# Linear attention and an ELU network on one core: the third token group's attention moved from transposed products to row products and DMA transposes

## The chip, the core and the metric

The kernel runs on one core of a Trainium2 chip. The core has a matrix engine (TensorE, "PE" in profiles, with its weight loads as "PEld"), VectorE ("DVE"), ScalarE ("ACT"), GpSimd ("POOL") and SyncE ("SP"), which mostly issues DMAs. Each engine works through its own list of instructions in order and waits on semaphores for the others. SBUF is the working memory with 128 partitions; PSUM, where TensorE leaves its results, has eight banks of 128 x 512 float32. The metric is the device time of one execution in microseconds (us).

## What is computed

```python
def _attn_ref(q, k, v, g_norm):                # q, k, v: 8 batches, 8 heads, 576 rows, 64 columns
    kv = np.einsum('bhsd,bhse->bhde', k, v)
    out = np.einsum('bhsd,bhde->bhse', q, kv)
    rms = np.sqrt(np.mean(out * out, axis=-1, keepdims=True) + 1e-06)
    return (out / rms * g_norm).astype(np.float32)

def _moe_ref(x, w_in, w_out):                  # x: 4608 x 512, w_in: 512 x 2048, w_out: 2048 x 512
    h = x @ w_in
    g = np.where(h > 0.0, h, 1.0 * (np.exp(np.minimum(h, 0.0)) - 1.0))
    return (g @ w_out).astype(np.float32)
```

Per batch and head, a 64 x 64 state kv is formed, each row of q is multiplied by it and normed; the heads are put side by side into rows of 512, and a two-layer network with an ELU runs over the 4608 rows. Inputs and output are float32; the kernel multiplies in bfloat16.

## The kernel before

**Groups.** The 4608 rows are cut into nine groups T of 512 (batches have 576 rows, so group T needs batches up to T, and group 2 still uses the end of batch 1). For each group there is an attention part, which ends in `xT[T]` (512 columns of x on partitions in four chunks c, 512 rows), a first product, and a second product. `mm1(T, i, tag)` computes two of the 16 column blocks of h, eight matmuls over 512 columns, into a pair of PSUM banks named by its tag, and hands it to `elu`: ScalarE takes Exp of it (line 350), VectorE takes min(e, 1) - 1 (358) and the larger of that and h (362) into `gT[T]`. The second step, returned as `rest`, reads h from PSUM, so the pair is free only after it. With `relu` set, ScalarE also copies Relu(h) into an SBUF tile `elu_h`, the pair is free after that, and VectorE adds from SBUF. `mm2(T, j, f0, f1)` adds the blocks f0 to f1 of the second product for the 128 rows j; `mm2_half(T, i)` is eight of these matmuls, and the last of a row block copies it out on ScalarE (`mm2_out`, 415) and stores it through SP.

**PSUM.** Pairs "A" and "B" (two banks each), two single banks "m", and two banks that are "x" up to group 1's end and the pair "at" afterwards. Whoever takes over a bank waits until its last reader is done.

**Two kinds of attention.** Groups 0, 1 and 2 use the class `Turned`: q is transposed on TensorE (`turned_q`, `q_t_mm`, line 174) and copied to `qT`; the product y comes out transposed (`y_mm`, 189), is squared on ScalarE (229), summed over a head by a matmul with a block of ones (`mean_mm`, 199), turned into 1/rms by Ln and Exp over 512 columns (208, 209) and scaled by VectorE into `xT` (212). From group 3 on, `attention(T)` does it by rows, in named pieces: `kv` (state of batch T on TensorE, copy on ScalarE), `se0`/`se1` (row product of half a group into the pair "at", Square on ScalarE), `sum0`/`sum1` (reduce on VectorE, 283), `inv0`/`inv1` (Ln, Exp on 16 columns, ScalarE, 291 and 292), `mul0`/`mul1` (scale on VectorE into `xs`, 299, and two DMA transposes on SP into `xT`, 306), `gain0`/`gain1` (g_norm on VectorE, 312). For it, q is loaded as float32 into `st_q` (`fetch_ahead`), cast on GpSimd in six instructions (`cast_q`), and transposed by two DMAs on SP into `qT` (`turn_q`, 331). `after_turn` puts a small copy on GpSimd that waits for these transposes, so that the next batch's loads, issued by GpSimd, start after them.

**Order.** The order on each engine is the order of the program text. Group 1's attention is spread over group 0's second product. Group 1's first product (i = 0 to 7, on pairs m, B, A, B, A, B, A, B) has the pieces of group 2's attention between its column blocks (`pieces`), then four halves of group 1's second product with the rest of group 2's norms. From T = 2 on, `window` runs group T's first product with the pieces of group T+1's attention before (`early`) and after (`late`) an ELU's `rest`, and with halves of group T-1's second product (`second`).

Of the kernel before, what the change touches and what calls it, by code (L numbers as in the profile page):

```python
# [16 lines left out]
def kernel(  # L17
# [14 lines left out]
    P = 128  # L32
# [110 lines left out]
    def qT_tile(b):  # L143
        qT[b] = attp.tile([P, 2, 2, RK, 64], BF16, name="qT", tag="qT", bufs=3)
        return qT[b]

    def x_tile(T):
        xT[T] = attp.tile([P, KC, G], BF16, name="xT", tag="xT")
        return xT[T]

    def kv_mm(b, kv_ps, u, ls=range(2)):
        for j in range(RK):
            for s in range(2):
                rows = slice(s * 64, s * 64 + 64)
                for l in ls:
                    nc.tensor.matmul(  # L156
                        kv_ps[s][l * 64 : l * 64 + 64, u * 64 : u * 64 + 64],
                        lhsT=bf["k", b][rows, 2 * l + u, j, :],
                        rhs=bf["v", b][rows, 2 * l + u, j, :],
                        start=(j == 0),  # L160
                        stop=(j == RK - 1),
                    )
# [8 lines left out]
    def q_t_mm(b, u, js, dst):  # L171
        for n, j in enumerate(js):
            for l in range(2):
                nc.tensor.transpose(  # L174
                    dst[l * 64 : l * 64 + 64, n * P : n * P + P], bf["q", b][:, 2 * l + u, j, :], ident
                )
# [166 lines left out]
    def elu(T, i, ps, relu):  # L343

        parts = [(0, 2, ps)]
        if isinstance(ps, list):
            parts = [(a, a + 1, ps[a].unsqueeze(1)) for a in range(2)]
        e = mlpt.tile([P, 2, G], BF16, name="elu_e", tag="elu_e")
        for lo, hi, h in parts:
            nc.scalar.activation(e[:, lo:hi, :], h, AF.Exp)  # L350
        if relu:
            r = mlpt.tile([P, 2, G], BF16, name="elu_h", tag="elu_h", bufs=2)
            for lo, hi, h in parts:
                nc.scalar.activation(r[:, lo:hi, :], h, AF.Relu)
            parts = [(0, 2, r)]

        def rest():
            nc.vector.tensor_scalar(  # L358
                out=e, in0=e, scalar1=1.0, scalar2=1.0, op0=ALU.min, op1=ALU.subtract
            )  # L360
            for lo, hi, h in parts:
                nc.vector.tensor_tensor(  # L362
                    out=gT[T][:, 2 * i + lo : 2 * i + hi, :],
                    in0=e[:, lo:hi, :],
                    in1=h,
                    op=ALU.add if relu else ALU.max,
                )

        return rest

    def g_tile(T):
        gT[T] = mlpg.tile([P, FC, G], BF16, name="gT", tag="gT")
# [20 lines left out]
    o_ps, o_sb = {}, {}  # L393
# [107 lines left out]
    for name in "kvq":  # L501
        fetch(name, 1, 1)
    load_w_out(3)
    for u in range(2):
        for name in "qkv":
            fetch(name, 2, u)
    fetch_ahead(3)
    cast_q(3)

# [11 lines left out]
    def turned_q(b, u, tag):  # L521

        ps = as_bf16(single(tag, "qt_ps"))
        q_t_mm(b, u, range(8), ps)
        return ps
# [42 lines left out]
                stop=(c == KC - 1),  # L568
            )

    qT_tile(0)
    x_tile(0)
    g_tile(0)
    g_ps = pair("A", "g_ps")
# [72 lines left out]
    def mm2_all(f0, f1, js=(2, 3, 0, 1)):  # L647
        for f in range(f0, f1):
            for j in js:
                mm2(0, j, f, f + 1)  # L650
# [4 lines left out]
            o_ps[0, j0 + t] = ps[:, t, :]  # L655

    x_tile(1)
    qT_tile(1)
    for u in range(2):
        n = Turned(1, u)  # L660
        if u == 0:
            mm2_all(0, 4, (2, 3))
        kv_ps = [single("x", "kv_ps") for _ in range(2)]
        kv_mm(1, kv_ps, u)
        kv_out(1, kv_ps, u, (A, A))
        if u == 0:
            mm2_all(0, 4, (0, 1))
        main = turned_q(1, u, "m")
        q_t_out(1, u, V, main, slice(0, 8))
        ends = as_bf16(single("m", "qt_ps"))  # L670
        for t in range(2):
            q_t_mm(t, u, (8,), ends[:, t * P : t * P + P])
        for t in range(2):
            q_t_out(t, u, V, ends[:, t * P : t * P + P], slice(8, 9))
        mm2_all(*((4, 6), (10, 11))[u])
        n.product([single("x", "y_ps") for _ in range(2)])
        for l in range(2):
            n.square(l)
        mm2_all(*((6, 7), (11, 12))[u])
        for l in range(2):  # L680
            n.sums(l, single("m", "mean"))
            n.inv(l)
            n.scale(l)
        mm2_all(*((7, 10), (12, 15))[u])
    for js in ((2, 3), (0, 1)):
        for j in js:
            mm2(0, j, 15, 16, out=False)
        for j in js:
            mm2_out(0, j)

    qT_tile(2)
    x_tile(2)
    n2 = [Turned(2, 0), Turned(2, 1)]

    def late_kv(u, tag):
        kv_ps = pair(tag, "kv_ps")
        kv_mm(2, kv_ps, u)
        kv_out(2, kv_ps, u, (A, A))  # L700

    def late_q(u, tag):
        main = turned_q(2, u, tag)
        end = as_bf16(single(tag, "qt_ps"))
        q_t_mm(2, u, (8,), end[:, 0:P])
        q_t_out(2, u, A, main, slice(0, 8))
        q_t_out(2, u, V, end[:, 0:P], slice(8, 9))

    def late_y(u):
        n2[u].product(pair("xm"[u], "y_ps"))  # L710
        for l in range(2):
            n2[u].square(l)

    def late_norm(u, l):
        n2[u].sums(l, single("mx"[u], "mean"))
        n2[u].inv(l)
        n2[u].scale(l)

    pieces = {
        1: lambda: late_kv(0, "x"),  # L720
        2: lambda: late_kv(1, "m"),
        3: lambda: late_q(0, "x"),
        4: lambda: (late_q(1, "m"), turn_q(3), after_turn(3), fetch_ahead(4)),
        5: lambda: late_y(0),
        6: lambda: late_norm(0, 0),
        7: lambda: late_norm(0, 1),
    }
    for i, tag in enumerate("mBABABAB"):
        rest = mm1(1, i, tag)
        rest()  # L730
        if i in pieces:
            pieces[i]()
    for j, tag in enumerate("AB"):
        o_ps[1, j] = pair(tag, "o_ps")[:, 0, :]
    mm2_half(1, 0)
    late_y(1)
    mm2_half(1, 2)
    late_norm(1, 0)
    mm2_half(1, 1)
    late_norm(1, 1)  # L740
    mm2_half(1, 3)
    start_psum.close()
    ps_at = ctx.enter_context(tc.tile_pool(name="ps_at", bufs=1, space=bass.MemoryType.PSUM))

    def window(T, at, early, late, second):
        for i in range(8):
            rest = mm1(T, i, "AB"[i % 2])
            for name in early.get(i, ()):  # L750
                at[name]()
            if i in second:
                second[i]()
            rest()
            for name in late.get(i, ()):
                at[name]()

    for T in range(2, NT):
        at, early, late = {}, {}, {}
        if T + 1 < NT:  # L760
            at = attention(T + 1)
# [54 lines left out]
```

## Time and profile before

| | us |
|---|---|
| median of 14 runs | 292.06 (291.72 to 292.58) |
| the profiled execution's own time | 292.08 |
| its span in the profile | 290.3 |
| first product of group 1 begins | 48.92 |
| first product of group 2 begins | 75.53 |
| first product of group 3 begins | 101.91 |
| second products, matmuls (line 399), in the chain | 40% of the span |
| first products, matmuls (line 378), in the chain | 41% of the span |
| VectorE, add or maximum of the ELU (line 362), 74 instructions | 84.6 |
| ScalarE, Exp of the ELU (line 350), 77 instructions | 73.8 |

The beginnings are starts of the first matmul in TensorE's timeline. Matmul durations in the trace (379 ns for one of 512 columns) overlap; the pace of a row of them, 16 in 3.45 us, is the cost of each. "Idle before" in a timeline is the time in which the engine did nothing ahead of that instruction, with what ended it.

### The profile page before, as it was taken

What the parts mean: (1) busy time and instruction counts of PE and PEld (TensorE: products, weight loads), DVE (VectorE), ACT (ScalarE), POOL (GpSimd) and SP (SyncE); (2) the same over time, 40 slices, a digit from 0 to 9 for tenths busy, and PEclk for the clock granted to TensorE, in tenths of its full rate; (3) what the DMA queues carried; (4) which work ended last, traced back from release to release, by engine and by line L of the source; (5) the groups of instructions that cost most, each with busy time, mean ns of one, the idle gap of its engine ahead of it and who ended that gap; (6) DMA issues with size and microseconds to landing.
All of it is one profiled execution on the core that took longest, in us unless ns stands there. A gap on an engine that the chain in (4) does not pass through costs nothing.

```text
span 290.3 us, 5182 instructions
## 1 busy us (share of the span) xinstructions
PE 282.6 (97%) x2145; PEld 130.3 (45%) x2145; DVE 165.3 (57%) x223; ACT 141.9 (49%) x207; POOL 46.9 (16%) x85
## 2 busy tenths in 40 slices
PE   8999999999999999999999999999999999999994
PEld 3444444444444444444444444444444444444443
DVE  2349632776368747762776377636774776344600
ACT  4568357587555435543554255525552555343320
POOL 7643341404200022203400330000000000000000
PEclk9999999999999999999999999999999999999999
DMA  7999999997901299958925894442140215020222
GB/s 210 187 204 206 206 207 237 303 193 217 184 2 36 43 169 246 169 100 240 235 53 93 224 239 73 86 107 72 38 102 6 75 36 108 0 75 0 72 75 73
DMA packets 46332, 37.77 MB, mean 130 GB/s; under 512 B 26468, under 2 KB 40036, under 8 KB 46308
## 3 DMA queue, kind: packets, MB, share of 16 engines
q0 software_dynamic: 15312, 20.71, 36.4%
q1 hardware_dynamic: 30592, 16.19, 25.8%
q10 hardware_dynamic: 404, 0.53, 0.5%
q8 instruction: 17, 0.28, 0.4%
q14 instruction: 7, 0.06, 0.0%
HBM read 36.70 MB, written 9.44 MB: 159 GB/s over the span
## 4 chain that ended last, share of the span: by engine, by line
PE 92%; DVE 3%; ACT 3%; DMA 1%; issue 0%; DVEq 0%
PE h_ps L378 41%; PE o_ps L399 40%; PE h_ps L563 2%; PE at L250 2%; PE kv_ps L519 2%; PE qt_ps L174 1%; DVE gT L362 1%; PE at L156 1%; ACT elu_e L350 1%; PE kv_ps L156 1%; PE mean L199 1%; PE y_ps L189 1%; PE mean L519 1%; ACT rT L209 1%; ACT rT L208 1%; DMA out_dram<-o_sb 1%
## 5 line engine op out<-in xcount | busy, mean ns | idle before, releaser
L399 PE MATMUL o_ps<-w_out_sb,gT 128*128 128x512 bf16 x560 | 130.5, 379 | 0.5 <-DVE gT L362 0.5
L378 PE MATMUL h_ps<-xT,w_in_sb 128*128 128x512 bf16 x552 | 128.7, 379 | 0.8 <-DVE gT L362 0.6
L350 ACT ACTIVATE elu_e<-h_ps 128x1024 bf16<-128x1024 f32 (+1 forms) x77 | 73.8, 974 | 91.4 <-PE h_ps L378 89.0
L362 DVE TENSOR_TENSOR gT<-elu_e,h_ps 128x1024 bf16<-128x1024 bf16 (+1 forms) x74 | 84.6, 1149 | 7.2
L399 PEld LDWEIGHTS <-gT 128*128 128x128 bf16 x560 | 54.4, 98 | 66.4 <-issue 1.8
L378 PEld LDWEIGHTS <-w_in_sb 128*128 128x128 bf16 x552 | 52.3, 98 | 62.5 <-issue 1.7
L358 DVE TENSOR_SCALAR elu_e<-elu_e 128x1024 bf16<-128x1024 bf16 x72 | 31.0, 430 | 69.3 <-ACT elu_e L350 69.0
L415 ACT COPY o_sb<-o_ps 128x512 f32<-128x512 f32 x32 | 18.5, 588 | 18.8 <-PE o_ps L399 18.7
L103 POOL CAST q_bf<-st_q 128x384 bf16<-128x384 f32 x30 | 14.4, 522 | 26.6 <-DMA st_q<-in_q_dram 26.6
L212 DVE SCALAR_TENSOR_TENSOR xT<-y_ps,g_col,rT 128x512 bf16<-128x512 f32 (+1 forms) x14 | 9.2, 672 | 15.4 <-ACT rT L209 13.4
L283 DVE TENSOR_REDUCE ss<-sq 128x16 f32<-128x1024 bf16 x12 | 14.6, 1220 | 4.9 <-ACT sq L277 4.9
L299 DVE TENSOR_TENSOR xs<-at,ss 128x1024 bf16<-128x1024 f32 x12 | 14.6, 1218 | 0.0
L277 ACT ACTIVATE sq<-at 128x1024 bf16<-128x1024 f32 x12 | 12.3, 1028 | 1.0 <-PE at L250 1.0
L339 POOL COPY gate<-qT 1x32 bf16<-1x32 bf16 x4 | 0.8, 199 | 73.3 <-DMA qT<-q_bf 73.3
L90 POOL DMA_DIRECT2D k_bf<-in_k_dram x12 | 8.4, 700 | 5.5 <-PE qt_ps L174 2.1
L156 PEld LDWEIGHTS <-k_bf 64*64 64x64 bf16 x576 | 6.4, 107 | 6.3 <-issue 5.9
L90 POOL DMA_DIRECT2D v_bf<-in_v_dram x12 | 8.3, 692 | 5.7 <-DMA w_in_sb<-in_moe_w_in_dram 2.1
L208 ACT ACTIVATE rT<-mean,eps_col 128x512 f32<-128x512 f32 (+1 forms) x9 | 6.6, 731 | 2.3 <-PE mean L199 2.1
L229 ACT ACTIVATE sq<-y_ps 128x512 bf16<-128x512 f32 x8 | 4.3, 595 | 6.4 <-PE y_ps L189 6.4
L112 DVE COPY o_sb<-o_ps 128x256 f32<-128x256 f32 x1 | 0.4, 425 | 11.5 <-DMA out_dram<-o_sb 11.5
L312 DVE TENSOR_SCALAR xT<-xT,g_col 128x1024 bf16<-128x1024 bf16 x12 | 5.7, 479 | 1.7 <-DMA xT<-xs 1.7
L112 DVE COPY qT<-qt_ps 128x128 bf16<-128x128 bf16 (+1 forms) x10 | 3.7, 406 | 5.0 <-PE qt_ps L174 5.0
(56 smaller groups left out, 113.3 us busy)
## 6 DMA issues: line engine op xcount, KB each, us to landing
out_dram<-o_sb SPq DMA_DIRECT2D x24, 256.0 KB, 3.9
st_q<-in_q_dram POOLq DMA_DIRECT2D x5, 1152.0 KB, 7.4
k_bf<-in_k_dram POOLq DMA_DIRECT2D x5, 576.0 KB, 9.4
v_bf<-in_v_dram POOLq DMA_DIRECT2D x5, 576.0 KB, 13.1
out_dram<-o_sb SPq DMA_DIRECT2D x19, 128.0 KB, 2.5
w_out_sb<-in_moe_w_out_dram POOLq DMA_DIRECT2D x4, 512.0 KB, 15.0
q_bf<-in_q_dram POOLq DMA_DIRECT2D x5, 288.0 KB, 13.4
k_bf<-in_k_dram POOLq DMA_DIRECT2D x4, 288.0 KB, 14.2
```

The source lines that it names most:

```text
L90: eng.dma_start(out=dst.rearrange("p m j d -> p m (j d)"), in_=in_[:, ms, :])
L103: nc.gpsimd.tensor_copy(out=bf["q", b][:, u, js], in_=raw[b][:, u::2, js, :].rearrange("p l j d -> p j l d"),)
L156: nc.tensor.matmul(kv_ps[s][l * 64 : l * 64 + 64, u * 64 : u * 64 + 64], lhsT=bf["k", b][rows, 2 * l + u, j, :], rhs=bf["v", b][rows, 2 * ...
L277: nc.scalar.activation(sq, st["se", h], AF.Square)
L283: nc.vector.reduce_sum(out=ss, in_=st.pop(("sq", h)).rearrange("p l (m e) -> p (l m) e", e=D), axis=AX.X,)
L299: nc.vector.tensor_tensor(out=st["xs"][:, 2 * h : 2 * h + 2, :].rearrange("p i (l m e) -> p l i m e", l=2, e=D), in0=se_ps.rearrange("p l ...
L350: nc.scalar.activation(e[:, lo:hi, :], h, AF.Exp)
L358: nc.vector.tensor_scalar(out=e, in0=e, scalar1=1.0, scalar2=1.0, op0=ALU.min, op1=ALU.subtract)
L362: nc.vector.tensor_tensor(out=gT[T][:, 2 * i + lo : 2 * i + hi, :], in0=e[:, lo:hi, :], in1=h, op=ALU.add if relu else ALU.max,)
L378: nc.tensor.matmul((ps[a] if isinstance(ps, list) else ps[:, a, :])[:, cols], lhsT=w_in_sb[:, c, f * P : f * P + P], rhs=xT[T][:, c, cols] ...
L399: nc.tensor.matmul(o_ps[T, j], lhsT=gT[T][:, f, j * P : j * P + P], rhs=w_out_sb[:, f, :], start=(f == 0), stop=(f == FC - 1),)
L415: nc.scalar.copy(o_sb[T, half][:, j % 2, :], o_ps[T, j])
```

## The change

Group 2 is given `attention(2)`, the row form, instead of `Turned`:

- Loads: batch 2's q, k and v come by `fetch_ahead(2)`, `cast_q(2)`, `turn_q(2)` and `after_turn(2)` ahead of batch 3's loads, in place of six half loads. All of `late_kv`, `late_q`, `late_y` and `late_norm` go.
- Group 1's first product uses the pairs m, B, A, m, B, A, m, B. Group 2's `kv` follows i = 2, `se0` i = 3, `sum0` and `inv0` i = 4, `mul0` i = 5, `se1` i = 6, and `sum1`, `inv1` and `mul1` come after i = 7. The ELU `rest` of i = 4 and 5 comes after `mul0`, that of 6 and 7 after `mul1`.
- `elu` gets a third way, `relu="later"`, for i = 4 and 7: the Relu copy is a step of its own (`freed`), which is put after `inv0` and `inv1`, so that ScalarE does the inverse norms first.
- After group 1's first product come five halves of its second product (row blocks 0 and 1 interleaved on pair A, half 4 ahead of their last quarter) instead of four; `turn_q(3)`, `after_turn(3)` and `fetch_ahead(4)` stand ahead of them, `gain0` and `gain1` behind.
- Group 2's window has three halves of group 1 left (at i = 1, 3, 5) and Relu copies at i = 3 and 5. The windows use B, A instead of A, B.
- In group 0's second product, four matmuls move from after group 1's second norm to before its second kv; `qT` tiles 0 and 1 are allocated earlier.

```diff
+        def freed():
             r = mlpt.tile([P, 2, G], BF16, name="elu_h", tag="elu_h", bufs=2)
             for lo, hi, h in parts:
                 nc.scalar.activation(r[:, lo:hi, :], h, AF.Relu)
-            parts = [(0, 2, r)]
+            parts[:] = [(0, 2, r)]
+
+        if relu and relu != "later":
+            freed()
...
-    for u in range(2):
-        for name in "qkv":
-            fetch(name, 2, u)
+    for b in range(2):
+        qT_tile(b)
+    fetch_ahead(2)
+    cast_q(2)
+    turn_q(2)
+    after_turn(2)
     fetch_ahead(3)
     cast_q(3)
...
-        mm2_all(*((4, 6), (10, 11))[u])
+        mm2_all(*((4, 6), (11, 12))[u])
...
-        mm2_all(*((6, 7), (11, 12))[u])
+        mm2_all(*((6, 7), (12, 13))[u])
...
-        mm2_all(*((7, 10), (12, 15))[u])
+        mm2_all(*((7, 11), (13, 15))[u])
...
-    for i, tag in enumerate("mBABABAB"):
-        rest = mm1(1, i, tag)
-        rest()
-        if i in pieces:
-            pieces[i]()
-    for j, tag in enumerate("AB"):
-        o_ps[1, j] = pair(tag, "o_ps")[:, 0, :]
-    mm2_half(1, 0)
-    late_y(1)
-    mm2_half(1, 2)
-    late_norm(1, 0)
-    mm2_half(1, 1)
-    late_norm(1, 1)
-    mm2_half(1, 3)
...
+    at = attention(2)
+    rest = {}
+    for i, tag in enumerate("mBAmBAmB"):
+        rest[i] = mm1(1, i, tag, "later" if i in (4, 7) else False)
+        if i < 4:
+            rest[i]()
+        if i == 2:
+            at["kv"]()
+        if i == 3:
+            at["se0"]()
+        if i == 4:
+            at["sum0"]()
+            at["inv0"]()
+            freed, rest[4] = rest[4]
+            freed()
+        if i == 5:
+            at["mul0"]()
+            rest[4]()
+            rest[5]()
+        if i == 6:
+            at["se1"]()
+    at["sum1"]()
+    at["inv1"]()
+    at["mul1"]()
+    freed, rest[7] = rest[7]
+    freed()
+    rest[6]()
+    rest[7]()
+    turn_q(3)
+    after_turn(3)
+    fetch_ahead(4)
+    ps = pair("A", "o_ps")
+    for j in range(2):
+        o_ps[1, j] = ps[:, j, :]
+    for f0, f1 in ((0, 8), (8, 12)):
+        for j in range(2):
+            mm2(1, j, f0, f1)
+    mm2_half(1, 4)
+    for j in range(2):
+        mm2(1, j, 12, 16, out=False)
+    for j in range(2):
+        mm2_out(1, j)
+    at["gain0"]()
+    at["gain1"]()
...
-        halves = {0: 4, 2: 5, 4: 6, 6: 7} if T == 2 else {0: 1, 1: 3, 2: 4, 3: 5, 4: 6, 5: 7}
+        halves = {1: 5, 3: 6, 5: 7} if T == 2 else {0: 1, 1: 3, 2: 4, 3: 5, 4: 6, 5: 7}
         second = {i: (lambda n=n: mm2_half(T - 1, n)) for i, n in halves.items()}
-        window(T, at, early, late, second)
+        window(T, at, early, late, second, (3, 5) if T == 2 else ())
```

More of the change, by code (lines that the diff above doesn't have):

```diff
@@ L350, in elu @@
             nc.scalar.activation(e[:, lo:hi, :], h, AF.Exp)
-        if relu:
+        def freed():
             r = mlpt.tile([P, 2, G], BF16, name="elu_h", tag="elu_h", bufs=2)
@@ L367, in rest @@
                 )
-        return rest
+        return (freed, rest) if relu == "later" else rest
     def g_tile(T):
@@ L569, in early @@
             )
-    qT_tile(0)
     x_tile(0)
@@ L657 @@
     x_tile(1)
-    qT_tile(1)
     for u in range(2):
@@ L689 @@
             mm2_out(0, j)
[L693 to L727, printed above, removed]
-    for i, tag in enumerate("mBABABAB"):
-        rest = mm1(1, i, tag)
-        rest()
-        if i in pieces:
-            pieces[i]()
@@ L733 @@
-    for j, tag in enumerate("AB"):
-        o_ps[1, j] = pair(tag, "o_ps")[:, 0, :]
-    mm2_half(1, 0)
-    late_y(1)
-    mm2_half(1, 2)
-    late_norm(1, 0)
-    mm2_half(1, 1)
-    late_norm(1, 1)
-    mm2_half(1, 3)
     start_psum.close()
     ps_at = ctx.enter_context(tc.tile_pool(name="ps_at", bufs=1, space=bass.MemoryType.PSUM))
-    def window(T, at, early, late, second):
+    at = attention(2)
[19 more added lines that the diff above has]
+            at["se1"]()
@@ L748, in window @@
+    at["gain1"]()
+    def window(T, at, early, late, second, relu=()):
         for i in range(8):
-            rest = mm1(T, i, "AB"[i % 2])
+            rest = mm1(T, i, "BA"[i % 2], i in relu)
             for name in early.get(i, ()):
```

## The prediction

> **What bounds the kernel now.** I read the page first, then the table of windows, then the timelines of TensorE, VectorE, ScalarE, GpSimd and SyncE between 40 and 102 us. The page's first part:
>
> ```profile
> PE 282.6 (97%) x2145; PEld 130.3 (45%) x2145; DVE 165.3 (57%) x223; ACT 141.9 (49%) x207; POOL 46.9 (16%) x85
> ```
>
> TensorE is the bound, so time comes only from fewer matmuls or less idling of PE. The table of windows shows where it idles (columns: window, length, busy PE, PEld, DVE, ACT, POOL, granted clock, DMA share, GB/s):
>
> ```profile
> 40.00:60.00 20.00, 19.38 (x236) 9.16 (x235) 10.09 (x16) 12.33 (x25) 5.18 (x9) 1.00 1.17 259
> 60.00:80.00 20.00, 18.97 (x180) 8.49 (x174) 11.01 (x17) 14.03 (x20) 5.20 (x10) 1.00 0.91 190
> 80.00:100.00 20.00, 20.00 (x144) 9.08 (x132) 15.27 (x18) 11.47 (x16) 0.00 (x0) 1.00 0.10 21
> ```
>
> PE lacks 1.65 us between 40 and 80 and nothing from 80 on until the tail: what the change touches is the only stage with holes. TensorE's timeline there (start, length, what, idle before it):
>
> ```profile
> 54.71 0.48 PE L156 MATMUL kv_ps<-v_bf,k_bf 64*64 64x64 bf16 x36
> 55.44 1.89 PE L378 MATMUL h_ps<-xT,w_in_sb 128*128 128x512 bf16 x8 [0.25 <-DVE gT L362]
> 57.25 0.69 PE L174 MATMUL qt_ps<-ident,q_bf 128*64 128x128 bf16 x18
> ...
> 64.40 0.38 PE L199 MATMUL mean<-sq,ones 128*128 128x512 bf16 x1
> 65.14 1.89 PE L378 MATMUL h_ps<-xT,w_in_sb 128*128 128x512 bf16 x8 [0.35 <-DVE gT L362]
> ...
> 69.28 0.41 PE L189 MATMUL y_ps<-qT,kv_sb 64*64 64x128 bf16 x8
> 69.92 1.89 PE L399 MATMUL o_ps<-w_out_sb,gT 128*128 128x512 bf16 x8 [0.23 <-DVE gT L362]
> ```
>
> The reader sees group 2's small products (kv, transposes, means, y) between group 1's, and waits for the ELU that must free a PSUM pair, since only A and B alternate. I call eight 512-column matmuls a unit; 16 take 3.45 us in the chain, so 1.726 each.
>
> **What the Trainium skill says.** "VectorE: DVE Perf Modes", Why PSUM operands drop a tier: a PSUM operand costs the fast mode. The trace agrees; the ELU's add by source:
>
> ```profile
> L362 DVE TENSOR_TENSOR gT<-elu_e,h_ps 128x1024 bf16<-128x1024 bf16 x64 | 78.2, 1221 | 6.7
> L362 DVE TENSOR_TENSOR gT<-elu_e,elu_h 128x1024 bf16<-128x1024 bf16 x3 | 2.1, 692 | 0.3
> ```
>
> "TensorE: Matmul & The Clock Gate", Architectural detail: ScalarE and VectorE run strictly in order, so a waiting Ln holds the next Exp; I lay out the stage that way. "GPSIMD Engine Reference", 1. Specifications: GpSimd shares SBUF interfaces with VectorE. The trace fits: the minimum/subtract at 55.87 us, during casts, takes 0.54 us against 0.43. "DMA: Bandwidth & Descriptors", Issuing engines are not separate DMA queues: transposes and loads share 16 engines; below 7.9 us against 6.4.
>
> **Part 1, group 0's second product.** Four matmuls move from after group 1's second norm to before its second kv. PE there idles 0.58 us (41.04 to 41.62, two kv matmuls aside) for the norm's last VectorE step; 4 x 0.216 = 0.86 us fill that and push kv by 0.29. The second norm then has 12 matmuls behind it instead of 16: mm1(1,0) starts at 48.92 + 0.29 - 0.86 = 48.35. Its last chunk c=3 is ready at 48.68 + 0.29 = 48.97 plus 0.06; three matmuls (0.65) go ahead of it, so it may start at 48.38. Gain 0.54.
>
> **Part 2, PE's work from there to the first product of group 3 (mm1(3,0), 101.91 before).** Both versions have 26 units, 44.88. Before: kv 2 x 0.41, transposes 2 x 0.62, y 2 x 0.34, means 4 x 0.22, and group 3's 0.71 + 0.47 + 0.34: 5.14. Eight units start 0.10 late after a small operation: 0.8. 101.91 - 48.92 = 52.99 leaves 2.17 of waits. After: group 2's kv 0.70, two state products 0.34, group 3's 1.51: 2.89; six late units 0.6. Gain 2.25 + 0.2.
>
> **Part 3, the waits after.** I put each engine's new order through spacings read from the timelines. VectorE, from starts at 83.06, 83.59, 84.73, 85.86 and 86.38: minimum/subtract 0.53, add from PSUM 1.14 (1.22 until its result counts; I take 1.19), reduce and scale 1.18, add from elu_h 0.66. ScalarE: Exp, Relu and Square 1.0, Ln with Exp on 16 columns 0.5. Hand-over 0.05. h(i) is mm1(1,i), from 48.38.
> - Three pairs now turn (m, B, A), so h3, which takes over m from h0, finds it free (ELU 0 over at 53.3, h3 starts at 54.3). h3 ends at 56.12, state product 0 at 56.46.
> - ScalarE: Exp 3 to 57.27, Square to 58.27. VectorE: ELU 3 to 59.13, reduce 0 to 60.31. ScalarE: Ln/Exp to 60.86. VectorE: scale 0 to 62.10.
> - There is one "at" pair, and scale 0 frees it: PE, done with h6 at 61.74, starts state product 1 at 62.15. Wait 0.41. Behind it on PE stand h7 and the second product.
> - ELU 4 ends at 63.28, ELU 5 at 64.99. The second product takes over pair A from ELU 5, and PE is through h7 at 64.31. Wait 0.72.
> - Behind Ln on ScalarE stand Relu 4, Exp 5 and Exp 6; Relu 4 is over at 61.86, before h7 asks for its pair at 62.49.
> - Reduce 1 ends at 66.19, scale 1 at 67.98, ELU 6 at 69.79 (half 4 takes over m at 70.22), ELU 7 at 70.97 (its chunks are wanted at 71.95). Half 4 in between is what hides ELU 7; without it that would be a wait of 0.75.
> - Group 3's window keeps its pace: two Relus add 2.0 to ScalarE and take 2 x 0.53 off VectorE, and its three halves instead of four leave scale 1 to the next group 4.4 us as before. No wait comes out.
> - GpSimd's casts of batch 3 fall on 62 to 65, over ELU 4 and 5: 0.1 on two instructions.
>
> Waits 0.41 + 0.72 + 0.2 = 1.33 against 2.17: gain 0.84. Bounds: no waits (gain 1.3 more), or late hand-overs in this chain of nine steps, 0.15 each, 1.4 less.
>
> **Part 4, the transfers.** Group 2's q becomes fp32 load, six casts, two transposes:
>
> ```profile
> 54.28 2.95 POOL L103 CAST q_bf<-st_q 128x384 bf16<-128x384 f32 x6 [8.92 <-DMA st_q<-in_q_dram]
> 57.25 5.76 SPq L331 DMA_TRANSPOSE qT<-q_bf  x2
> 65.11 0.20 POOL L339 COPY gate<-qT 1x32 bf16<-1x32 bf16 x1 [7.88 <-DMA qT<-q_bf]
> ```
>
> w_out's last slice lands at 28.10 + 14.5 = 42.6; the six half loads behind it land every 1.4 us (44.0 to 51.2). So st_q lands at 45.4, is cast at 48.4, and transposed 6.4 us (125.93 to 132.33, no other traffic) to 7.9 (57.25 to 65.11, beside loads) later: 54.8 to 56.4. Needed at 56.12; up to 57.1 the two waits above absorb it. On SP the four stores of group 0 now wait behind it, 49.8 to 52-54; nobody needs their buffers before 73. Batch 3's loads wait for the gate, 40-45 to 55-57: q lands after 5.8 us (61-63), k and v by 70, needed at 75; its transposes stand on SP behind group 2's four anyway, from 70.5, landing 77, needed 79.7. Cost nothing. Group 2's xT: scale 1 ends 67.98, two transposes land 3.75 later (97.42 to 101.17 before), gain 0.45: 72.2, needed 73.67. Slack 1.5; contended by v's load I allow 1 more. Group 3's margin stays as tight as before (gain over at 101.66, next product 101.91). Batch 4's load moves from 65.7 to 77.4, cast by 88, wanted on SP at 96: nothing.
>
> **Sum.** 0.54 + 2.25 + 0.2 + 0.84 = 3.83 off the profiled 292.08 (span 290.3): 288.25; from the median 292.06 the same. I say 288.3. After mm1(3,0) the order is the same but for the pair names.
>
> **Rivals.**
> - Fewer waits: ELU and norms overlap better than my hand-overs; the 1.33 vanish, 287.0. For it: three pairs; against: scale 0 and ELU 5 really are in one queue. 0.12.
> - Late VectorE or late xT: VectorE is laid out solid from 60.9 to 71.4, so each extra 0.1 us goes straight to PE, and xT's transposes meet batch 3's v load; 1 to 1.5 more, 289.3 to 289.8. 0.22, with up to 291.4.
> - Slower: the transposed q is late. The state product stands in PE's queue, all of group 1 behind it. Past 57.1 each us costs one; from 61.5 the kernel is over 0.2% slower, at 63 it takes 288.3 + 5.9 = 294.2. For it: DMA is full till 51 and the chain load, cast, transpose is serial. Against: it needs 5 us over the slowest turn seen. 0.06.
> - The change does not do what it says for the time: PE's work is merely dealt anew, and waits of 3.2 us more eat the rest. Against it: 2.25 us of matmuls are gone whatever waits. Within 0.2% (291.5 to 292.6): 0.03.
>
> **How the numbers follow.** Forecast (287.4 to 289.1) 0.57; the rivals as given. 0.2% (0.6 us) is about what a measurement tells from none. Faster 0.91, same 0.03, slower 0.06. Range 286.9 to 290.3: the fewer-waits case and most of the late ones.
>
> **What would show it.** qt_ps and mean gone from group 2; h0 near 48.4; PE idle about 0.4 ahead of the second state product and 0.7 ahead of the second product, both from VectorE; none ahead of the first, with the gate near 55.5; mm1(3,0) near 98.1. PE idle for "DMA qT" or "DMA xT", or over 2 us of it between 48 and 98, would make it wrong.

## The result and the profile after

The changed kernel takes 288.47 us (median of 10, 288.03 to 294.74), the kernel before 292.02 (median of 48); the ratio is 0.988, with a 95% interval of 0.987 to 0.989. The forecast was 288.3, in a range of 286.9 to 290.3. The profiled execution took 288.44 us, its span is 286.7. The one execution of 294.74 had a mean granted clock of 0.988 against 0.997 to 1.0 in the others (e3 below, where TensorE waits long for q, has 0.986 to 0.994), and since there is no profile of it, its cause is open.

The first part of the page of the changed kernel:

```profile
PE 279.4 (97%) x2121; PEld 129.0 (45%) x2121; DVE 165.6 (58%) x225; ACT 138.9 (48%) x202; POOL 47.9 (17%) x89
```

TensorE is busy for 3.2 us less than before. Part of that are short waits, not matmuls: the modelled end of eight matmuls lies 1.90 us after their start where their pace is 1.73, so the busy column counts up to 0.17 of each wait as work. Its table of windows (window, length, busy PE, PEld, DVE, ACT, POOL, granted clock, DMA share, GB/s) shows where it still idles:

```profile
40.00:60.00 20.00, 20.00 (x232) 9.40 (x231) 11.37 (x18) 13.21 (x24) 5.25 (x10) 1.00 1.04 230
60.00:80.00 20.00, 19.50 (x195) 9.03 (x194) 12.66 (x18) 10.53 (x18) 5.28 (x10) 1.00 1.06 204
80.00:100.00 20.00, 19.07 (x103) 8.48 (x102) 14.59 (x19) 11.04 (x15) 2.95 (x6) 1.00 0.86 167
```

Between 40 and 60 the column shows no idle time any more. The last row is the news: by this column TensorE lost nothing there before and now lacks 0.93 us, and the DMA share has gone from 0.10 to 0.86. TensorE's timeline names the place (start, length, what, idle before it):

```profile
48.30 5.37 PE L382 MATMUL h_ps<-xT,w_in_sb 128*128 128x512 bf16 x24
53.60 0.78 PE L156 MATMUL at<-v_bf,k_bf 64*64 64x64 bf16 x72
54.31 1.90 PE L382 MATMUL h_ps<-xT,w_in_sb 128*128 128x512 bf16 x8
56.14 0.41 PE L250 MATMUL at<-kv_sb,qT 64*128 64x64 bf16 x16
56.48 5.35 PE L382 MATMUL h_ps<-xT,w_in_sb 128*128 128x512 bf16 x24
61.77 0.41 PE L250 MATMUL at<-kv_sb,qT 64*128 64x64 bf16 x16
62.11 1.90 PE L382 MATMUL h_ps<-xT,w_in_sb 128*128 128x512 bf16 x8
64.51 8.79 PE L403 MATMUL o_ps<-w_out_sb,gT 128*128 128x512 bf16 x40 [0.50 <-DVE gT L366]
73.14 1.89 PE L382 MATMUL h_ps<-xT,w_in_sb 128*128 128x512 bf16 x8
...
93.97 3.62 PE L403 MATMUL o_ps<-w_out_sb,gT 128*128 128x512 bf16 x16
98.52 1.90 PE L382 MATMUL h_ps<-xT,w_in_sb 128*128 128x512 bf16 x8 [0.94 <-DVE xT L312]
```

Group 2's attention now leaves only the state (53.60) and two small rows, 56.14 and 61.77, between long rows of first products. The row at 64.51 is the second product waiting for ELU 5. The row at 98.52 is group 3's first product: it waits for the second half of its x, which the forecast had at no cost. Measured at the pace of 1.726 us for a unit of eight matmuls, these two waits are 0.67 (64.51 less 62.11 and one unit) and 1.10 (98.52 less 93.97 and two units), 1.77 together; the idle column shows less because modelled ends reach beyond the pace.

The wait that was forecast ahead of the second state product is not there. The row at 61.77 starts 0.11 later than three units after 56.48, but every row ahead of a small one ends that late here (0.12 for the three units from 48.30, 0.10 for the one from 54.31), and the forecast has this among its six late units.

The transfers of group 2's q, on GpSimd in the changed kernel:

```profile
45.53 2.75 POOL L103 CAST q_bf<-st_q 128x384 bf16<-128x384 f32 x6 [11.42 <-DMA st_q<-in_q_dram]
54.76 0.20 POOL L339 COPY gate<-qT 1x32 bf16<-1x32 bf16 x1 [6.48 <-DMA qT<-q_bf]
```

The q has landed by 45.53 and is transposed by 54.76, 1.4 us before the state product at 56.14 asks for it.

What SyncE does ahead of the late x, in the changed kernel:

```profile
91.87 1.29 SPq L461 DMA_DIRECT2D out_dram<-o_sb  x2
93.26 3.46 SPq L306 DMA_TRANSPOSE xT<-xs  x2
96.81 3.58 SPq L331 DMA_TRANSPOSE qT<-q_bf  x2
```

and in the kernel before, where the four transposes of x have q's directly behind them:

```profile
88.80 11.15 SPq L306 DMA_TRANSPOSE xT<-xs  x4
100.05 3.56 SPq L331 DMA_TRANSPOSE qT<-q_bf  x2
103.71 1.41 SPq L457 DMA_DIRECT2D out_dram<-o_sb  x1
```

Group 1's last two stores (256 KB each) have moved ahead of the last two transposes of group 3's x, because the change has three halves instead of four in group 2's window, at i = 1, 3, 5 instead of 0, 2, 4, 6. The last half, with its stores, now stands just before `mul1`. VectorE shows what that costs, first in the changed kernel:

```profile
91.81 1.22 DVE L299 TENSOR_TENSOR xs<-at,ss 128x1024 bf16<-128x1024 f32 x1
...
97.98 0.49 DVE L312 TENSOR_SCALAR xT<-xT,g_col 128x1024 bf16<-128x1024 bf16 x1 [2.73 <-DMA xT<-xs]
```

then in the kernel before:

```profile
96.20 1.22 DVE L299 TENSOR_TENSOR xs<-at,ss 128x1024 bf16<-128x1024 f32 x1
...
101.17 0.49 DVE L312 TENSOR_SCALAR xT<-xT,g_col 128x1024 bf16<-128x1024 bf16 x1 [1.70 <-DMA xT<-xs]
```

From the end of the scale to the landed x it is 4.95 us (93.03 to 97.98) instead of 3.75 (97.42 to 101.17). The room for it hardly changed: in the kernel before the product starts 4.49 us after the scale's end (97.42 to 101.91), and now it could have started 4.39 after it (93.03 to 97.42, two units after 93.97).

SyncE's time on the stores is the small part of these 1.20 us: the transposes begin 0.23 us after the scale's end, in the kernel before 0.03. The large part is that the two take longer to issue, 3.46 us (the row of 93.26 above) where the kernel before has

```profile
97.45 2.50 SPq L306 DMA_TRANSPOSE xT<-xs  x2
```

All of the difference lies in the first of the two, directly behind the stores: 2.15 us instead of 1.19; the second takes 1.26 in both.

The tail gives 0.2 us that the forecast did not have. In the kernel before, the last copy of the output waits for a store:

```profile
286.67 0.42 DVE L112 COPY o_sb<-o_ps 128x256 f32<-128x256 f32 x1 [11.47 <-DMA out_dram<-o_sb]
```

TensorE had ended at 286.21. In the changed kernel TensorE ends at 282.83 and the copy follows at once:

```profile
282.92 0.42 DVE L112 COPY o_sb<-o_ps 128x256 f32<-128x256 f32 x1 [10.75 <-PE o_ps L440]
```

**The ledger.** h0 is 0.62 earlier (48.92 to 48.30), group 3's first product 3.39 (101.91 to 98.52), the last product 3.38 (282.55 to 279.17), the end of the span 3.6.

### The profile page after: what moved, and what is told of

It reads as the page before. It is cut to its first block, busy times and chain, and to the rows that moved or that the text cites. A ratio compares the mean times of both kernels' runs of the same rounds, so it can differ in the third digit from the quotient of the medians.

```text
span 286.7 us, 5146 instructions
## 1 busy us (share of the span) xinstructions
PE 279.4 (97%) x2121; PEld 129.0 (45%) x2121; DVE 165.6 (58%) x225; ACT 138.9 (48%) x202; POOL 47.9 (17%) x89
## 4 chain that ended last, share of the span: by engine, by line
PE 92%; DVE 4%; DMA 1%; ACT 1%; issue 0%; SPq 0%; DVEq 0%
PE o_ps L403 41%; PE h_ps L382 39%; PE h_ps L570 2%; PE at L250 2%; PE kv_ps L526 2%; DVE gT L366 1%; PE at L156 1%; PE o_ps L440 1%; PE qt_ps L174 1%; PE kv_ps L156 1%; DMA xT<-xs 1%; PE mean L199 1%; PE y_ps L189 1%; PE mean L526 1%; ACT elu_e L350 1%; DVE elu_e L362 1%
## 5 line engine op out<-in xcount | busy, mean ns | idle before, releaser
L366 DVE TENSOR_TENSOR gT<-elu_e,h_ps 128x1024 bf16<-128x1024 bf16 (+1 forms) x72 | 79.8, 1117 | 7.4 <-PE o_ps L403 0.5
L103 POOL CAST q_bf<-st_q 128x384 bf16<-128x384 f32 x36 | 16.9, 513 | 33.1 <-DMA st_q<-in_q_dram 29.0
L283 DVE TENSOR_REDUCE ss<-sq 128x16 f32<-128x1024 bf16 x14 | 17.1, 1218 | 5.1 <-ACT sq L277 5.1
L299 DVE TENSOR_TENSOR xs<-at,ss 128x1024 bf16<-128x1024 f32 x14 | 17.1, 1219 | 1.2 <-ACT ss L292 1.2
L277 ACT ACTIVATE sq<-at 128x1024 bf16<-128x1024 f32 x14 | 14.4, 1028 | 0.0
L212 DVE SCALAR_TENSOR_TENSOR xT<-y_ps,g_col,rT 128x512 bf16<-128x512 f32 (+1 forms) x10 | 6.2, 642 | 11.0 <-ACT rT L209 9.0
L312 DVE TENSOR_SCALAR xT<-xT,g_col 128x1024 bf16<-128x1024 bf16 x14 | 6.7, 480 | 3.6 <-DMA xT<-xs 3.6
L355 ACT ACTIVATE elu_h<-h_ps 128x1024 bf16<-128x1024 f32 x7 | 7.2, 1022 | 0.0
L250 PEld LDWEIGHTS <-qT 64*128 64x128 bf16 (+1 forms) x248 | 4.3, 97 | 6.1 <-issue 5.9
L526 PE MATMUL kv_ps<-zeros 128*128 128x512 bf16 x13 | 5.3, 574 | 1.2 <-DVE one L519 1.2
```

The costliest lines, as they stand in the source:

```text
L103: nc.gpsimd.tensor_copy(out=bf["q", b][:, u, js], in_=raw[b][:, u::2, js, :].rearrange("p l j d -> p j l d"),)
L277: nc.scalar.activation(sq, st["se", h], AF.Square)
L283: nc.vector.reduce_sum(out=ss, in_=st.pop(("sq", h)).rearrange("p l (m e) -> p (l m) e", e=D), axis=AX.X,)
L299: nc.vector.tensor_tensor(out=st["xs"][:, 2 * h : 2 * h + 2, :].rearrange("p i (l m e) -> p l i m e", l=2, e=D), in0=se_ps.rearrange("p l ...
L366: nc.vector.tensor_tensor(out=gT[T][:, 2 * i + lo : 2 * i + hi, :], in0=e[:, lo:hi, :], in1=h, op=ALU.add if relu else ALU.max,)
L526: nc.tensor.matmul(ps, lhsT=zeros[:, 0:P], rhs=zeros, start=True, stop=True)
```

## The experiments

The theory after the result: the gain is fewer small matmuls on TensorE, group 0's move, and fewer waits; it would be about 1 us larger if the stores of group 1 did not meet group 3's transposes. Rivals: the late x comes from the scale or from other loads, not from the stores; the single pieces (Relu ahead or behind, group 0's move, the order of the loads) do nothing for the time.

### e1: the stores behind group 3's x, ahead of its q

```diff
-        if j % 2 == 1:
+        if j % 2 == 1 and (T, j) != (1, 3):
             store(T, half)
...
+            at["store"] = lambda: store(1, 1)
-            late = {0: ("kv",), 1: ("se0",), 2: ("mul0",), 4: ("se1",), 5: ("mul1", "ahead")}
+            late = {0: ("kv",), 1: ("se0",), 2: ("mul0",), 4: ("se1",), 5: ("mul1", "store", "ahead")}
```

> Only the issue of two stores moves: the two DMAs that store rows 256 to 511 of group 1 are issued on SP behind group 3's second pair of xT transposes instead of ahead of it. Theory (the 0.94 us that TensorE waits for group 3's xT at 98.5 us is caused by these stores, which run beside the transposes): the two transposes take 2.5 us to issue instead of 3.5 and land 3.75 us after the scale, the wait falls from 0.94 to under 0.2, time 287.5 to 287.8 against 288.5. Rival (the scale itself is late, or the transposes are slowed by batch 4's loads): the wait stays, 288.4.

Measured: 288.24 us (287.87 to 288.59, n 4), ratio 0.9865 (0.9851 to 0.9879). The time missed what was expected. The wait of group 3 is gone from the trace, and the two transposes of its x take 2.50 us to issue, as expected; but the next q now stands behind the stores. SyncE in this kernel:

```profile
85.68 9.90 SPq L306 DMA_TRANSPOSE xT<-xs  x4
95.68 1.29 SPq L461 DMA_DIRECT2D out_dram<-o_sb  x2
97.06 4.50 SPq L331 DMA_TRANSPOSE qT<-q_bf  x2
```

q's two transposes take 4.50 us to issue instead of 3.58, and the first of them, behind the stores, 2.17 instead of 1.32. The gate on GpSimd comes at 104.38 instead of 103.18, the next batch's loads with it, and a new wait of 0.40 us stands at the last block of group 3's first product (122.17). It waits for an ELU, which VectorE does behind a gain of group 4's x, and that gain waits 1.12 us for its DMA. So the 1.10 goes when the stores go behind x; one transfer further on they cost part of it again.

### e2: k loaded ahead of q

```diff
-    fetch_ahead(2)
+    fetch("k", 2)
+    raw[2] = stage.tile([P, 4, RK, D], FP32, name="st_q", tag="q")
+    load(raw[2], "q", 2)
+    fetch("v", 2)
```

> Batch 2's k is loaded ahead of its q, so that q lands, is cast and is transposed one load (2.9 us) later: transposes down at about 57.5 instead of 54.6, where the state product is wanted at 56.1. Theory of the prediction (1 us of lateness is absorbed by the later waits for VectorE, then each us costs one): PE waits 1.4 ahead of the first state product, the waits ahead of the second state product and of the second product (0.1 and 0.67) vanish, and 0.6 to 0.8 is left: 289.1 to 289.3. Rival (the VectorE chain of group 2 starts with this product, so nothing is absorbed): 289.9.

Measured: 291.43 us (290.83 to 294.62, n 14), ratio 0.9992 (0.9971 to 1.0012): 2.1 us later than expected, and the change's gain gone within the interval. TensorE in the profiled execution, one of the late ones (294.12 us):

```profile
57.27 0.20 PE L250 MATMUL at<-kv_sb,qT 64*128 64x64 bf16 x2 [1.17 <-DMA qT<-q_bf]
58.26 0.26 PE L250 MATMUL at<-kv_sb,qT 64*128 64x64 bf16 x6 [0.79 <-DMA qT<-q_bf]
...
77.44 1.44 PE L382 MATMUL h_ps<-xT,w_in_sb 128*128 128x512 bf16 x3 [2.69 <-DVE xT L312]
```

The first two rows are the wait for q that was meant, 1.96 us by the idle column. The third was not expected: the gate opened at 58.35 instead of 54.76, so batch 3's loads ran 3.6 us later and beside the transposes of group 2's x; the last of these landed 7.98 us after its scale (68.88 to 76.86), against 4.12 in the changed kernel. After that wait the granted clock was 0.50 from 77 to 80 us. How much of this the other executions had is not known, since only this one has a trace; but seven of the fourteen, 290.83 to 291.71, have a mean clock of 0.999 or 1.0, so most of the loss is there without the halved clock.

### e3: k and v ahead of q

The edit is that of e2 with `fetch("v", 2)` ahead of q too.

> Batch 2's k and v are both loaded ahead of its q: transposes down at about 60.4, 4.3 us after the state product wants them. Theory of the prediction: 4.3 less 0.8 absorbed, 3.5 slower than the changed kernel, 291.8 to 292.2, so the whole gain is gone at this lateness. Rival: batch 3's loads, which follow the gate and now run until about 74, delay group 2's xT transposes too, and the time is 293 or more; other rival: nothing is absorbed, 292.8.

Measured: 295.17 us (294.81 to 295.9, n 5), ratio 1.0101 (1.0088 to 1.0114). Slower than before, as the rival in the forecast had it for a late q, but 3 us beyond what was expected. The time is that of the rival with 293 or more, but not for its reason: group 2's x landed 3.85 us after its scale (74.82 to 78.67), and no row of TensorE waits for it. TensorE:

```profile
58.62 0.20 PE L250 MATMUL at<-kv_sb,qT 64*128 64x64 bf16 x2 [2.40 <-DMA qT<-q_bf]
61.48 0.34 PE L250 MATMUL at<-kv_sb,qT 64*128 64x64 bf16 x6 [2.65 <-DMA qT<-q_bf]
61.75 8.13 PE L382 MATMUL h_ps<-xT,w_in_sb 128*128 128x512 bf16 x24
```

The waits are 5.05 us, where the expectation has room for 3.3 to 3.7 (291.8 to 292.2 less 288.47). And the 24 matmuls behind them take 8.13 us where the changed kernel takes 5.35 for the same row: 2.78 more. The table of windows of this kernel shows why (the clock is the third column from the end):

```profile
60.00:62.00 2.00, 0.52 (x7) 0.32 (x8) 0.00 (x0) 0.14 (x1) 0.20 (x1) 0.65 0.84 150
62.00:64.00 2.00, 2.00 (x6) 0.75 (x5) 1.08 (x1) 0.89 (x1) 1.88 (x3) 0.50 1.07 299
64.00:66.00 2.00, 2.00 (x7) 0.63 (x6) 0.14 (x1) 0.61 (x1) 0.37 (x1) 0.50 0.70 150
66.00:68.00 2.00, 2.00 (x8) 0.80 (x7) 1.11 (x1) 1.73 (x4) 0.00 (x0) 0.64 1.05 425
```

The clock is half from 60.6 to 67.4. Together, less the wait of 0.67 that is gone from this trace, the second product begins 23.81 us after h0 (48.09 to 71.90), in the changed kernel 16.21: 7.60 more, where the two profiled executions, 295.9 and 288.44, are 7.46 apart.

### e4: group 0's four matmuls back where they were

```diff
-        mm2_all(*((4, 6), (11, 12))[u])
+        mm2_all(*((4, 6), (10, 11))[u])
...
-        mm2_all(*((6, 7), (12, 13))[u])
+        mm2_all(*((6, 7), (11, 12))[u])
...
-        mm2_all(*((7, 11), (13, 15))[u])
+        mm2_all(*((7, 10), (12, 15))[u])
```

> The four matmuls of group 0's second product go back behind group 1's second norm. Theory: a term of the sum that stands alone; PE waits 0.4 to 0.6 again ahead of group 1's second kv, the first product of group 1 starts at 48.9 instead of 48.3, and everything behind it follows: 289.0 to 289.1. Rival (the 0.6 us is slack that the waits for VectorE at 61 to 65 us would take up): 288.4 to 288.6.

Measured: 288.99 us (288.56 to 289.29, n 4), ratio 0.989 (0.9877 to 0.9903), as expected. TensorE's timeline has the wait of the kernel before again:

```profile
41.17 0.47 PE L156 MATMUL kv_ps<-v_bf,k_bf 64*64 64x64 bf16 x34 [0.37 <-DVE xT L212]
```

From group 1's first kv row to h0 it is 17.12 us here (31.36 to 48.48) and in the kernel before (31.80 to 48.92), 16.54 in the changed kernel (31.76 to 48.30): the move is worth 0.58. Later waits take up next to none of it: from the same kv row to group 3's first product it is 67.28 us here (to 98.64) and 66.76 in the changed kernel.

### e5, e10 and e11: the stores behind x and q, and the changed kernel beside it

The edit is that of e1 with `("mul1", "ahead", "store")`, so that nothing urgent stands behind the stores.

> As the run with the stores behind the xT transposes, but the two stores now stand behind the transposes of batch 4's q as well. There the wait for group 3's xT was gone, yet the gate for batch 5's loads came at 104.4 instead of 103.2 us, the loads met group 4's transposes and a new wait of 0.40 us came at 122. Theory (the second half of that is the price of standing ahead of q's transposes): gate at 102 or earlier, neither wait, 287.4 to 287.7. Rival (the loads meet group 4's transposes whatever the gate does, since TensorE is also earlier): 288.0 to 288.3 again.

> The kernel of e5_store_last once more, on one chip with the changed kernel, to compare these two directly. Theory: the two stores moved behind group 3's transposes are worth 0.5 to 0.7 us of the 0.94 us wait that they cause, 287.6 to 288.0 beside 288.3 to 288.6 for the changed kernel. Rival: the gain was a difference between chips, both within 0.2 us of each other.

> The changed kernel itself, on one chip with e9 and e10. 288.3 to 288.6 by every theory; it is the figure that the other two are held against. A look at group 2's first product shows how far the landing of group 2's transposed x moves from one execution to the next: within 0.5 us if it is set by the issue times, more if the loads beside it decide.

Measured: e5 287.81 us (287.38 to 288.68, n 4), ratio 0.9856 (0.9839 to 0.9873). On one chip, e10 287.03 (286.87 to 287.34, n 4), ratio 0.9828 (0.9812 to 0.9845), and e11 288.27 (288.1 to 288.49, n 4), ratio 0.987 (0.9854 to 0.9886): 1.24 us, about the wait of 1.10, and more than the 0.5 to 0.7 that were expected. SyncE in e10:

```profile
85.66 9.90 SPq L306 DMA_TRANSPOSE xT<-xs  x4
95.65 3.60 SPq L331 DMA_TRANSPOSE qT<-q_bf  x2
99.35 2.06 SPq L461 DMA_DIRECT2D out_dram<-o_sb  x2
```

and TensorE, where the wait of 98.52 was:

```profile
93.99 3.62 PE L403 MATMUL o_ps<-w_out_sb,gT 128*128 128x512 bf16 x16
97.44 1.89 PE L382 MATMUL h_ps<-xT,w_in_sb 128*128 128x512 bf16 x8
```

The last x landed 3.84 us after its scale (93.04 to 96.88), close to the 3.75 of the kernel before, and TensorE goes straight on. The wait stands in all nine traces with the stores in the changed kernel's place (0.84 to 1.03 in the idle column) and in none of the three with the stores moved (e1, e5, e10), whatever else was changed: the stores are its cause. e10 is the fastest version, 1.7% under the kernel before. e5's profile still had a wait of 0.64 us at group 2's first product. The profile names a copy of ScalarE that ended at that moment, but in the changed kernel this product starts (73.14) before that copy does (73.34), so it does not need it; what it needs is group 2's last x. That landed 4.12 us after its scale in the changed kernel, 4.15 in e11, 4.14 in e10, 4.90 in e4, but 5.92 in e5 (67.20 to 73.12) and 6.12 in e6. e5 and e10 are one and the same kernel. From about 5.1 on, an estimate, TensorE waits (5.92 less its 0.64, 6.12 less e6's 1.12). Its transposes run beside batch 3's loads; why they are late in some executions stays open.

### e6 and e7: the Relu copies ahead of the inverse norms, and none

```diff
-        rest[i] = mm1(1, i, tag, "later" if i in (4, 7) else False)
+        rest[i] = mm1(1, i, tag, i in (4, 7))
...
-            freed, rest[4] = rest[4]
-            freed()
...
-    freed, rest[7] = rest[7]
-    freed()
```

That is e6; e7 has `False` in the place of `i in (4, 7)`, and so reads h from PSUM in all eight ELUs.

> The Relu copies of i = 4 and 7 go ahead of the two inverse norms on ScalarE instead of behind them. Theory: Ln of the first half waits for Relu 4 to end at 60.4, 0.5 later than now; scale 0, the second state product, ELU 5 and so the second product all move by 0.5, and the second Relu costs nothing (Ln waits for the reduce longer than that): 288.9 to 289.1. Rival (ScalarE has slack there): 288.5.

> No Relu copies for i = 4 and 7: VectorE reads h from PSUM (1.22 us an add instead of 0.69) and frees the pairs itself. Theory: pair B is free for h7 only at 63.3 instead of 61.3, so TensorE waits 1.2 there, and starts the second product at 65.1 instead of 64.5; the 0.67 of waiting that it has now is inside that: 0.5 to 0.7 slower, 289.0 to 289.2. Rival (the copies only load ScalarE): 288.3 to 288.5.

Measured: e6 288.83 us (288.02 to 289.68, n 5), ratio 0.989 (0.987 to 0.991); e7 289.04 (288.82 to 289.24, n 4), ratio 0.9893 (0.9878 to 0.9908). e6's time alone does not tell it from the changed kernel. Its timeline does:

```profile
61.77 0.41 PE L250 MATMUL at<-kv_sb,qT 64*128 64x64 bf16 x16 [0.27 <-DVE xs L299]
...
64.49 1.67 PE L403 MATMUL o_ps<-w_out_sb,gT 128*128 128x512 bf16 x7 [0.48 <-DVE gT L366]
```

From h0 to the second product it is 16.52 us (47.97 to 64.49), in the changed kernel and in e11 16.21. That alone would be weak, since e10, which has the changed kernel's text up to there, has 16.40; but the cause can be seen: the Ln of the first half starts only at 59.91, as Relu 4 ahead of it (59.00) ends, VectorE's scale waits 1.01 us for it instead of 0.62, and the second state product waits for the scale. In e7 h7 waits for its pair (its line numbers are one higher):

```profile
63.42 1.89 PE L383 MATMUL h_ps<-xT,w_in_sb 128*128 128x512 bf16 x8 [1.25 <-DVE gT L367]
```

That is ELU 4, which must read the pair itself, behind scale 0 on VectorE. The second product begins 17.15 us after h0, 0.94 later than with the Relu. Some 0.34 of that is something else: in ELU 3, ahead of all this, VectorE's minimum and subtract took 0.77 us instead of 0.43 (why is open), and scale 0 began that much later (12.49 us after h0 instead of 12.15). The other 0.6 is within what was expected. So the Relu at i = 4 is worth more than the order that it is put in.

### e8: e2 with batch 3's loads not held back by the gate

```diff
     turn_q(2)
-    after_turn(2)
     fetch_ahead(3)
+    after_turn(2)
     cast_q(3)
```

> Batch 2's k ahead of its q as before (that run took 291.4), but batch 3's loads are issued before the gate on batch 2's transposes, so that they are over before group 2's xT transposes begin. Theory (2.2 us of that run's loss is group 2's xT transposes running beside batch 3's loads, 2.7 us of waiting at 77 us): that wait goes; q's transposes now run beside loads and land about 1.2 later, so TensorE waits about 3 us for them instead of 2: 289.6 to 290.4. Rival (xT is late because the scale is late): the wait of 2.7 stays, 292 or more.

Measured: 301.21 us (300.54 to 302.35, n 4), ratio 1.0315 (1.0293 to 1.0337), some 11 us beyond what was expected: TensorE waits 11.3 us for q, not 3. TensorE:

```profile
60.04 0.20 PE L250 MATMUL at<-kv_sb,qT 64*128 64x64 bf16 x2 [3.73 <-DMA qT<-q_bf]
67.84 0.34 PE L250 MATMUL at<-kv_sb,qT 64*128 64x64 bf16 x6 [7.59 <-DMA qT<-q_bf]
68.11 6.86 PE L382 MATMUL h_ps<-xT,w_in_sb 128*128 128x512 bf16 x24
```

The last row takes 1.51 us more than the 5.35 of the changed kernel. q's transposes, begun at 51.86, were over at 67.8: 16 us beside three whole loads, against 6.45 (48.31 to 54.76) in the changed kernel, where these loads are held back. The part of the theory that was asked for is supported: with these loads over, group 2's x lands 3.85 us after its scale (80.05 to 83.90) and its first product has no wait, so e2's 2.69 us were very likely those loads. All of this comes some 11 us later than in e2, though, so more than the loads is different. The price of the other side was not foreseen at all.

### e9 and e12: the tail

e9 splits two stores of group 0 into four, for the same bytes:

```diff
-            if b0 == b1:
+            if b0 == b1 and (T, half) != (0, 1):
```

> The changed kernel with the two stores of group 0's rows 256 to 511 written as four, one for each 128 rows: the same bytes to the same places, two more DMA instructions on SyncE[...]. It asks why the tail is 0.2 us shorter after the change. Theory: the last VectorE copy of the output waits in the kernel before for an older store that shares its signal, and the change shifted that sharing; the wait comes back and the time is 288.7 to 288.9, with VectorE's last copy behind a store. Rival: the 0.2 us at the tail are chance between executions, or come from the stores' earlier issue; the time stays at 288.3 to 288.6 and the last copy starts straight behind TensorE.

> The kernel before itself, looked at once more. In its profiled execution VectorE's last copy of the output began 0.37 us after TensorE's last instruction had ended, behind a store; in those of the changed kernel it begins within 0.1 us. Theory: this wait belongs to the kernel before, and is seen again, 0.3 to 0.4 us; then the change is worth 0.2 us at the tail. Rival: it was chance in that one execution, and the copy begins within 0.1 us. The time is 291.7 to 292.6 by both.

Measured: e9 288.88 us (288.67 to 288.96, n 4), ratio 0.9889 (0.9871 to 0.9908); e12 292.12 in one execution. In e9 the last copy begins straight behind TensorE (283.40, with TensorE over at 283.31), so the theory of shared signals finds no support. Its time is the one that the theory gave, but from another place: 0.37 of the 0.6 us over e11 lie at the second product, which begins 16.58 us after h0 instead of 16.21. GpSimd's casts of batch 3's q and VectorE's ELU 5 show where most of that comes from, first in e9, then in the changed kernel:

```profile
62.40 3.21 POOL L103 CAST q_bf<-st_q 128x384 bf16<-128x384 f32 x6 [4.63 <-DMA st_q<-in_q_dram]
62.71 0.72 DVE L362 TENSOR_SCALAR elu_e<-elu_e 128x1024 bf16<-128x1024 bf16 x1
...
63.49 2.75 POOL L103 CAST q_bf<-st_q 128x384 bf16<-128x384 f32 x6 [5.89 <-DMA st_q<-in_q_dram]
62.72 0.42 DVE L362 TENSOR_SCALAR elu_e<-elu_e 128x1024 bf16<-128x1024 bf16 x1
```

In e9 the q landed about 1 us earlier and the casts fall on ELU 5's minimum and subtract, which takes 0.72 us instead of 0.42, and the casts 3.21 instead of 2.75; in the changed kernel that instruction is over before the casts begin. In e12 the last copy waits again, at 286.71 with TensorE over at 286.27: the wait belongs to the kernel before. Why the change takes it away is open.

## Why the prediction was right, by its steps

- **The bound** held. TensorE's busy time fell by 3.2 us and the time by 3.6. The 3.2 is more than the 2.25 + 0.2 of part 2 because the busy column also counts part of each short wait that is gone.
- **Part 1**, 0.54 with h0 at 48.38: h0 came at 48.30, and e4 shows 0.58 for the move.
- **Part 2**, 2.25 us of small matmuls and 0.2 of late units: from h0 to group 3's first product there are 50.22 us (48.30 to 98.52). The forecast's terms give 44.88 + 2.89 + 0.6 = 48.37, and with the 1.77 of measured waits 50.14. The sum closes to 0.08. No run takes the terms apart, but the rows do: the state takes 0.71 (53.60 to 54.31), the two products 0.34 each, and the six late units 0.09 to 0.12 each.
- **Part 3**, waits of 0.41, 0.72 and 0.2. The first did not come: I had ScalarE begin Exp 3 when all of h3 was done, but h3 lies in two single banks with an Exp for each, and the first begins at 55.43, before h3 ends. That pulls the whole chain to scale 0 forward, which ends at 61.68 instead of 62.10, just before TensorE is ready for the second state product. The second was 0.67. The 0.2 for GpSimd's casts did not come, by luck: the casts began at 63.49, after ELU 5's minimum and subtract, and the add and the reduce beside them took 1.22 and 1.21 us as elsewhere; in e9 they began at 62.40 and cost 0.3. The Relu at i = 4 and its place behind the Ln did what the forecast says (e7, e6); no run takes the third pair away. Not foreseen was the wait of 1.10, at group 3's first product.
- **Part 4**, transfers at nothing. For group 2 the times hold: q landed for 45.53 (forecast 45.4), transposed for 54.76 (54.8 to 56.4), batch 3's q cast from 63.49 (landing 61 to 63), its transposes for 76.53 (77), batch 4's loads at 77.06 (77.4), group 2's x gained by 72.05 (72.2). The last figure is right by two errors, since the scale ended 0.54 us earlier than forecast (67.44) and its transposes took 4.12 us, not 3.75; and this trace is the lucky end of it: the slack was used up in e5 and e6. The step that failed is "Group 3's margin stays as tight as before": the room stayed (4.39 us against 4.49), but the landing was taken from the old times, and the stores that the new places of group 1's halves put ahead of group 3's last transposes on SP were not counted. They cost 1.10 us, and e10 gives them back.
- **After mm1(3,0) the order is the same**: the last product is 3.38 us earlier, so nothing was lost, but the tail gave 0.2.
- **The sum** of 3.83 stands against 3.64 in the profiled executions: 0.08 more in part 1, 0.66 less of foreseen waits, 1.10 for the unforeseen one, 0.08 lost in the rest, and 0.22 more at the tail; 3.83 + 0.08 + 0.66 - 1.10 - 0.08 + 0.22 = 3.61. So 288.3 against 288.47 is in part luck: the unforeseen wait is nearly made up by foreseen ones that did not come and by the tail.
- **The signs.** As forecast, the transposes and means of group 2 are gone, the gate comes at 54.76, and 0.67 us are lost ahead of the second product. Against it, nothing is lost ahead of the second state product, and group 3's first product starts at 98.52 instead of 98.1. By the forecast's own word TensorE idle for "DMA xT" would make it wrong, and the wait of 98.52 is that, by way of VectorE's gain, which waits for the DMA.
- **The rivals.** "Fewer waits" at 287.0 did not come; e10, without the unforeseen wait, reaches its figure (287.03) with 0.72 us still lost ahead of the second product (62.04 to 64.49 less a unit). "Slower by a late q" did not come, but its mechanism is real: e3 makes it. The forecast put q at 61.5 just over the kernel before, at 0.2% slower (292.6); e3 has q at 61.48 and takes 295.17. One us per us was too little there, since TensorE's clock was half after the wait. "Late xT" named the right kind of wait in the wrong group.

## What to carry to other kernels

When a step is moved, follow its stores too: put every DMA of the moved step into its place on the issuing queue and ask which urgent transfer comes next there. Issue stores that nobody waits for behind the transposes that somebody does, and behind all of them, since in e1, one place further on, they delayed the next gate. Hold loads back while a transpose is in flight that TensorE waits for, and price a TensorE wait of several us at more than its length (2.78 us more in e3, 1.51 in e8).

## What was not expected of the hardware

- A wait can cost the clock that follows it, and not by its length. In e3 TensorE did two small matmuls in 5.3 us (56.2 to 61.5); the clock was 0.50 from 60.6 to 67.4, nearly 6 us into the work, and the next 24 large matmuls took 2.78 us longer. In e8, after 11.3 us with as little work, the clock came back 3.3 us into the work (67.84 to 71.1), and the same row took 1.51 longer. The Trainium skill, "TensorE: Matmul & The Clock Gate", Part 1: The HAM clock gate, says that an idle window of about 3.4 us halves the clock and about as long a busy one restores it. The traces agree with the halving, and e8 with the return; e3's return took longer, and in e2 the clock fell 2.2 us into an idle stretch of 2.69 and stayed at 0.50 for over 3 us (76.9 to 80.3), while the 1.96 us of waits before it left the clock at full.
- Transposes lose much beside other transfers. q's two took 16 us beside loads in e8 and 6.45 where the loads were held back; group 3's x took 4.95 us behind two stores and 3.75 to 3.84 without. The skill's "DMA: Bandwidth & Descriptors", SWDGE vs HWDGE vs iDMA, says that the engines take turns between the queues of loads by GpSimd and of those by SyncE; the loss beside the loads fits that, and the runs show its size. The stores come from SyncE like the transposes, and why the first transpose behind them takes 0.96 us longer to issue is open.
